# Windowed attention and a squared-ReLU feed-forward: scores by 64-query steps in place of 128-query halves

## The chip, the cores and the metric

One core of a Trainium2 chip runs the whole program. TensorE does the matrix products and writes them to PSUM, ScalarE (ACT) and VectorE (DVE) read PSUM and work between buffers, GpSimd (POOL) and SyncE (SP) issue transfers; a transfer from main memory or a transposing transfer runs on the 16 DMA engines. The metric is the time of one execution on the device in microseconds (us). The kernel before takes 302.01 us (median of 3 runs, 301.80 to 302.15).

## What is computed

Eight sequences with eight heads, 576 positions of 64 numbers. Each query sees the keys at most 32 positions away; the attention output, heads side by side, is the input of a feed-forward layer with a squared ReLU.

```python
B, H, S, D = 8, 8, 576, 64
scores = np.matmul(q, k.transpose(0, 1, 3, 2)) / np.sqrt(D)
scores = np.where(np.abs(pos[:, None] - pos[None, :]) <= 32, scores, -1e9)
attn = softmax(scores)                       # over the keys
x = np.matmul(attn, v)                       # to (B*S, H*D) = (4608, 512)
h = x @ w_in                                 # (512, 2048)
out = np.maximum(h, 0) ** 2 @ w_out          # (2048, 512), float32 out
```

## The kernel before

**Attention by groups.** A group is 192 queries of one sequence, all eight heads; there are 24 groups (`NG`, L15), G = 3 b + g. Its keys are the 256 positions from 32 before to 32 after it. Queries and keys stand transposed in `QT` and `KT`: head dimension on the partitions, heads in four columns `j`, the even head of a pair in partitions 0 to 63 and the odd one (`par`) in 64 to 127. The 256 keys are cut in two halves of 128 (`w`). The 192 queries are three steps of 64: step 0 needs the first key half, step 2 the second, and the middle step needs 64 keys of each.

`scores` (L534) computes, for each key half and head, 128 keys by 128 queries (L565): for `w` = 0 the middle step and then step 0 (an access pattern with a negative step, L564), for `w` = 1 the middle step and then step 2. That is 16 matmuls of 128 columns, in eight pairs: the two of a pair use the lower and the upper 64 rows of the array. From the fourth group on (`NSPLIT = 3`) one block of 16 does both halves and fills all four banks of the PSUM tile `AT`, 1024 columns for each half. ACT takes the exponential of each half, 128 x 1024, into `E` (L589); DVE multiplies it by a band mask of zeros and ones, broadcast over the heads, into `PT` (L594). The masks `MASK[0..3]` are 128 x 128: 1 is the usual second half, 2 and 3 serve the ends of a sequence.

`pv` (L598) multiplies the transposed probabilities by the values: for each key half eight matmuls (L622), one a head, with `PT` as the loaded weights and 65 columns of `V` as the moving operand. Column 64 of `V` is 1, so the sum of the weights comes out beside the result. Head h writes columns `65 * y` to `65 * y + 64` of a bank. Half 0 is divided out for step 0 (DVE L641 and L644, into `XA`), then those rows are set to zero (L650) and half 1 adds to the middle step and makes step 2 (L641 and L644, into `XB`). `VS = 66` is the width in which `V` is stored, two columns of ones.

`xturn` (L652) turns `XA` and `XB` into `XT` with transposing transfers on the SP queue (L717, L720) from group 3 on. The queries and keys of sequences 2 to 7 come by POOL transfers (L394) and are turned by SP transfers (L524); those loads wait for the second P V block of the group three earlier (`gate`, L381).

**The feed-forward.** `mm1` (L725) computes 128 hidden rows by n tokens (192, 256, then 512) in four matmuls each (L737); ACT applies the ReLU (L743) and DVE squares (L746). `mm2` (L750) adds 16 products of 128 x 512 for 128 tokens (L757); ACT moves the result out (L767) and issues the store (L769).

**The order.** Every piece is recorded with its readers and writers, a key and an assumed duration (`Prog.rec`, L96). `schedule` (L127) plays the program through once with these durations: an engine takes, of the pieces that are ready, the one with the lowest key. What it finds is the fixed order in which each engine gets its instructions; on the chip semaphores keep the dependencies. So a changed duration or dependency of one piece can move other pieces, transfers on the queues too. At the start, idle matmuls of zeros (L322) are put into TensorE's gaps.

## Time and profile before

| what | value |
|---|---|
| runs, median | 302.01 us |
| profiled execution, first to last instruction | 299.9 us |
| outside the span (start, end, difference of executions) | 2.1 us |
| TensorE matmul, busy | 291.9 us, 97% |
| DVE, busy | 167.2 us, 56% |
| ACT, busy | 160.3 us, 53% |
| POOL, busy | 107.1 us, 36% |
| DMA engines, mean busy share | nine tenths or more in most of the first 30 of 40 slices |

How to read it: the page has one time per instruction, and "busy" of an engine is the time in which at least one of its instructions is under way. A matmul's time runs to its modelled end, so it holds the passage through the array, and several overlap: a 512-column matmul lasts 379 ns while the next one starts 216 ns after it. What a matmul costs in a row of matmuls is therefore the distance between starts, which the timeline gives: it merges like instructions and shows the start of the first, the time to the end of the last, and their number.

### The profile page before, as it was taken

What the parts mean: (1) busy time and instruction counts of PE and PEld (TensorE: products, weight loads), DVE (VectorE), ACT (ScalarE), POOL (GpSimd) and SP (SyncE); (2) the same over time, 40 slices, a digit from 0 to 9 for tenths busy, and PEclk for the clock granted to TensorE, in tenths of its full rate; (3) what the DMA queues carried; (4) which work ended last, traced back from release to release, by engine and by line L of the source; (5) the groups of instructions that cost most, each with busy time, mean ns of one, the idle gap of its engine ahead of it and who ended that gap; (6) DMA issues with size and microseconds to landing.
All of it is one profiled execution on the core that took longest, in us unless ns stands there. A gap on an engine that the chain in (4) does not pass through costs nothing.

```text
span 299.9 us, 6209 instructions
## 1 busy us (share of the span) xinstructions
PE 291.9 (97%) x2394; PEld 171.8 (57%) x2431; DVE 167.2 (56%) x385; ACT 160.3 (53%) x250; POOL 107.1 (36%) x143
## 2 busy tenths in 40 slices
PE   7899999999999999999999999999999999999996
PEld 3578866848677767664544454444544444444445
DVE  6898775737674767563656666665666632222100
ACT  3497834836467656750765476536744643443312
POOL 8993336503544354455256335533500000000000
PEclk9999999999999999999999999999999999999999
DMA  9999999997999999999999999999992120100112
GB/s 169 176 206 184 196 177 174 169 176 137 164 169 165 95 162 146 155 138 186 180 168 131 114 166 156 125 149 156 154 128 70 55 61 35 37 35 35 38 70 105
DMA packets 160636, 39.83 MB, mean 133 GB/s; under 512 B 149984, under 2 KB 156128, under 8 KB 160608
## 3 DMA queue, kind: packets, MB, share of 16 engines
q0 software_dynamic: 106016, 17.93, 89.3%
q1 hardware_dynamic: 49264, 12.14, 28.5%
q10 hardware_dynamic: 5328, 9.37, 9.1%
q8 instruction: 19, 0.31, 0.5%
q14 instruction: 9, 0.07, 0.1%
HBM read 36.70 MB, written 9.44 MB: 154 GB/s over the span
## 4 chain that ended last, share of the span: by engine, by line
PE 90%; DMA 5%; POOL 3%; issue 1%; ACT 0%; POOLq 0%; ACTq 0%
PE ht L737 41%; PE outp L757 40%; DMA w<-in_moe_w_in_dram 5%; PE at L622 4%; PE at L565 4%; POOL v L443 1%; POOL w L456 1%; PE at L485 1%; PE ht L782 1%; PE outp L782 1%; POOL kpair L426 1%; POOL qpair L426 1%; ACT rt L743 0%; ACT oe L792 0%; POOL dif L325 0%
## 5 line engine op out<-in xcount | busy, mean ns | idle before, releaser
L737 PE MATMUL ht<-xt,w 128*128 128x256 bf16 (+2 forms) x885 | 140.0, 302 | 1.3 <-DMA w<-in_moe_w_in_dram 0.5
L757 PE MATMUL outp<-w,gt 128*128 128x512 bf16 x536 | 133.0, 379 | 1.3
L743 ACT ACTIVATE rt<-ht 128x512 bf16<-128x512 f32 (+1 forms) x152 | 85.9, 578 | 87.1 <-PE ht L737 85.1
L737 PEld LDWEIGHTS ht<-xt,w 128*128 128x128 bf16 x896 | 81.3, 98 | 43.8 <-ACT rt L743 0.6
L746 DVE TENSOR_TENSOR gt<-rt 128x512 bf16<-128x512 bf16 (+1 forms) x152 | 61.5, 408 | 61.6 <-ACT rt L743 60.0
L757 PEld LDWEIGHTS outp<-w,gt 128*128 128x128 bf16 x560 | 51.9, 98 | 54.1 <-ACT oe L767 1.0
L394 POOL DMA_DIRECT2D kraw<-in_k_dram x36 | 27.7, 778 | 107.3 <-PE at L622 56.8
L589 ACT ACTIVATE e<-at 128x1024 bf16<-128x1024 f32 x46 | 44.8, 1021 | 8.7 <-PE at L565 8.4
L594 DVE TENSOR_TENSOR pt<-e,mask 128x1024 bf16<-128x1024 bf16 x46 | 31.8, 691 | 29.0 <-ACT e L589 28.9
L443 POOL DMA_DIRECT2D v<-in_v_dram x48 | 38.2, 809 | 0.0
L767 ACT ACTIVATE oe<-outp 128x512 f32<-128x512 f32 x35 | 21.1, 604 | 29.6 <-PE outp L757 29.6
L394 POOL DMA_DIRECT2D qraw<-in_q_dram x36 | 27.7, 778 | 0.0
L622 PEld LDWEIGHTS at<-v,pt 128*128 128x128 bf16 x384 | 18.3, 98 | 9.9 <-DMA v<-in_v_dram 0.6
L622 PE MATMUL at<-v,pt 128*128 128x65 bf16 x384 | 20.1, 194 | 0.5 <-ACT pt L586 0.5
L644 DVE TENSOR_TENSOR xa<-at,rs 64x512 bf16<-64x512 f32 x24 | 16.7, 695 | 0.9
L644 DVE TENSOR_TENSOR xb<-at,rs 128x512 bf16<-128x512 f32 x24 | 16.5, 689 | 0.7
L565 PEld LDWEIGHTS at<-qt,kt 64*128 64x128 bf16 x384 | 10.8, 94 | 8.7 <-issue 7.1
L565 PE MATMUL at<-qt,kt 64*128 64x128 bf16 x384 | 15.2, 217 | 0.2
L641 DVE RECIPROCAL rs<-at 64x8 f32<-64x8 f32 (+1 forms) x48 | 10.0, 209 | 9.1 <-PE at L622 7.7
L650 DVE MEMSET at<- 64x520 f32 x23 | 11.3, 492 | 3.5 <-DVE xa L644 2.6
L450 DVE COPY v<-v 64x512 bf16<-64x512 bf16 x16 | 5.9, 372 | 5.1 <-PE ht L737 2.9
L789 DVE COPY oe<-ht 128x128 f32<-128x128 f32 x1 | 0.3, 292 | 14.5 <-PE ht L782 14.5
(67 smaller groups left out, 83.2 us busy)
## 6 DMA issues: line engine op xcount, KB each, us to landing
out_dram<-oe ACTq DMA_DIRECT2D x35, 256.0 KB, 3.2
qraw<-in_q_dram POOLq DMA_DIRECT2D x36, 96.0 KB, 5.8
w<-in_moe_w_in_dram POOLq DMA_DIRECT2D x4, 512.0 KB, 10.7
v<-in_v_dram POOLq DMA_DIRECT2D x16, 128.0 KB, 6.6
w<-in_moe_w_out_dram POOLq DMA_DIRECT2D x4, 512.0 KB, 18.8
v<-in_v_dram POOLq DMA_DIRECT2D x16, 96.0 KB, 7.0
kraw<-in_k_dram POOLq DMA_DIRECT2D x12, 112.0 KB, 4.6
kraw<-in_k_dram POOLq DMA_DIRECT2D x12, 96.0 KB, 4.9
```

What stands on the lines that cost most here:

```text
L394: self.p.rec("POOL", lambda e, j=j: e.dma_start(raw[0:h, j, :].rearrange("p (h d) -> p h d", h=8), s[:, j]), writes=[("raw", t, G % NRAW, ...
L443: self.p.rec("POOL", lambda e, j=j, lo=lo, hi=hi, k0=k0: e.dma_start(vt[lo - k0:hi - k0, j, :, 0:64], self.v[b, :, lo:hi, :].rearrange("h ...
L565: mm = e.matmul(sc[:, 512 * par + 128 * j:512 * par + 128 * j + 128], kt[r:r + 64, j, k0:k0 + 128], q, start=G >= NBIAS, stop=True, skip_g ...
L589: self.p.rec("ACT", lambda e, e_=e_, sc=sc: e.activation(e_[:], sc, ACTF.Exp, scale=0.125), reads=tags[w], writes=[("e", n % 2)], key=key, ...
L594: self.p.rec("DVE", lambda e, pt=pt, ee=ee, mb=mb: e.tensor_tensor(pt[:], ee, mb, ALU.mult), reads=[("e", n % 2), ("mask", mi)], writes=[( ...
L622: mm = e.matmul(avp[:, c:c + 65], pt[:, 4 * (h % 2) + h // 2, :], vt[:, w, h, 0:65], start=(w == 0 and y == 0), stop=True, skip_group_chec ...
L644: self.p.rec("DVE", lambda e: e.tensor_tensor(x[r0:128, :].rearrange("p (x y c) -> p x y c", x=2, y=4), av[:, :, :, 0:64], rb, ALU.mult), ...
L737: mm = e.matmul(ht[:, n * x:n * x + n], self.W1[:, ft, 128 * d:128 * d + 128], self.XT[:, ft, r:r + n], start=(ft == 0), stop=(ft == 3))
L743: self.p.rec("ACT", lambda e: e.activation(rt[:, 0:c], ht[:, 0:c], ACTF.Relu), reads=[f"ht{k % 2}"], writes=[("rt", k % 4)], key=key, dur= ...
L746: self.p.rec("DVE", lambda e: e.tensor_tensor(gt[:, d0:d0 + len(ds), r:r + n], rr, rr, ALU.mult), reads=[("rt", k % 4)], writes=[("gt", s, ...
L757: mm = e.matmul(op[:], gt[:, d, r:r + 128], self.W2[:, d, :], start=(d == 0), stop=(d == 15))
L767: self.p.rec("ACT", lambda e: e.activation(oe, op[:], ACTF.Copy), reads=[f"outp{u % 2}"], writes=[("oe", u % 4)], key=key, dur=act(512), n ...
```

## The change

From the fourth group on the scores are computed by `scores_steps` instead of `scores`: for each of the three 64-query steps and each head, the 128 keys of that step by 64 queries. That is 24 matmuls of 64 columns in 12 pairs, steps 0 and 2 into the first two banks of `AT`, the middle step into 256 columns each of the other two. ACT takes two exponentials, 128 x 1024 for steps 0 and 2 (into `E`) and 128 x 512 for the middle step (into `E1`). DVE makes one masked product of 1024 columns, which puts step 0 and step 2 into the right half of their tile of `PT`, and two of 512 columns over 64 partitions, which move the upper and the lower 64 keys of the middle step to the partitions where `pv` wants them: keys 0 to 63 of the middle step go to partitions 64 to 127 of half 0, keys 64 to 127 to partitions 0 to 63 of half 1. `pv` of half 0 now waits for the first product and the first of the small ones, half 1 for the first product and the second small one.

`PT` becomes two buffers with both halves in place of three with one half, used by groups in turn; the four masks become slices of one tensor, so that one access pattern reaches two of them. `pv` uses all 66 columns of `V` in all groups, and the memset of L650 clears 2 x 264 columns in place of 2 x 260. The planner's duration of a score block becomes 590 (`SDUR`), before 660.

```diff
+    def scores_steps(self, G):
...
+        def f(e):
+            for s in (0, 2, 1):
+                for j in range(4):
+                    for par in range(2):
+                        r = 64 * par
+                        c = 512 * par + (1024 + 64 * j if s == 1 else 128 * j + 32 * s)
+                        mm = e.matmul(self.AT[:, c:c + 64], kt[r:r + 64, j, a + 64 * s:a + 64 * s + 128],
+                                      qt[r:r + 64, j, a + 64 * s:a + 64 * s + 64], start=True, stop=True, skip_group_check=True)
+            return mm
...
+        self.moe = self.p.rec("PE", f, reads=rd, writes=lo + hi, key=key, dur=SDUR, name=f"S{G}B")
+        e2, e1, pt = self.E[n], self.E1[n], self.PT[n]
+        self.p.rec("ACT", lambda e: e.activation(e2[:], self.AT[:, 0:1024], ACTF.Exp, scale=0.125), reads=lo, writes=[("e", n)],
+                   key=key, dur=act(1024), name=f"X{G}A")
+        mid = self.AT[:, 1024:2048].rearrange("p (x c) -> p x c", x=2)[:, :, 0:256]
+        self.p.rec("ACT", lambda e: e.activation(e1[:].rearrange("p (x c) -> p x c", x=2), mid, ACTF.Exp, scale=0.125), reads=hi,
+                   writes=[("e1", n)], key=key, dur=act(512), name=f"X{G}B")
+        m0, m2 = 2 if g == 0 else 1, 3 if g == 2 else 1
+        out = bass.AP(pt, 64, [[2048, 128], [128, 8], [1024, 2], [1, 64]])
+        mb = bass.AP(self.MK, 128 * m0 + 64, [[512, 128], [0, 8], [128 * (m2 - m0), 2], [1, 64]])
+        self.p.rec("DVE", lambda e: e.tensor_tensor(out, e2[:].rearrange("p (h s q) -> p h s q", h=8, s=2), mb, ALU.mult),
+                   reads=[("e", n), ("mask", m0), ("mask", m2)], writes=[("pt", n, 0, 0), ("pt", n, 1, 0)], key=key, dur=dve(1024),
+                   name=f"M{G}A")
+        for w in range(2):
+            r, x = 64 * w, 64 * (1 - w)
+            mm = bass.AP(self.MK, r * 512 + 128 + 64, [[512, 64], [0, 8], [1, 64]])
+            self.p.rec("DVE", lambda e, w=w, r=r, x=x, mm=mm: e.tensor_tensor(
+                pt[x:x + 64, w, :, 0:64], e1[r:r + 64, :].rearrange("p (h q) -> p h q", h=8), mm, ALU.mult),
+                reads=[("e1", n), ("mask", 1)], writes=[("pt", n, w, 1)], key=key + 0.01 * w, dur=dve(512), name=f"M{G}m{w}")
...
     def pv(self, G, w):
...
-                c = c0 + 512 * x + 65 * y
-                mm = e.matmul(avp[:, c:c + 65], pt[:, 4 * (h % 2) + h // 2, :], vt[:, w, h, 0:65], start=(w == 0 and y == 0),
+                c = c0 + 512 * x + VS * y
+                mm = e.matmul(avp[:, c:c + VS], pt[:, 4 * (h % 2) + h // 2, :], vt[:, w, h, :], start=(w == 0 and y == 0),
                               stop=True, skip_group_check=True)
...
-        rd = [("v", G % NV, w), ("vset", G % NV), ("pt", n % 3), "zz"]
+        rd = [("v", G % NV, w), ("vset", G % NV), ("pt", G % 2, w, 0), ("pt", G % 2, w, 1), "zz"]
...
-            z = avp[64:128, c0:c0 + 1024].rearrange("p (x c) -> p x c", x=2)[:, :, 0:260]
+            z = avp[64:128, c0:c0 + 1024].rearrange("p (x c) -> p x c", x=2)[:, :, 0:4 * VS]
...
-            for ws in ((0,), (1,)) if G < NSPLIT else ((0, 1),):
+            for ws in ((0,), (1,)) if G < NSPLIT else ():
                 at(3 * G - LEAD + 0.3 * ws[0], self.scores, G, ws)
+            if G >= NSPLIT:
+                at(3 * G - LEAD, self.scores_steps, G)
```

More of the change, by code (lines that the diff above doesn't have):

```diff
@@ L67 @@
 ESPLIT = 0
+SDUR = 590
 IOTA = -1
@@ L297, in alloc @@
         self.DIF = sb("dif", [128, 128], F32)
-        self.MASK = [sb(f"mask{i}", [128, 128], BF16) for i in range(4)]
+        self.MK = sb("mask", [128, 4, 128], BF16)
+        self.MASK = [self.MK[:, i, :] for i in range(4)]
         self.ID = sb("ident", [128, 128], BF16)
         self.E = [sb(f"e{i}", [128, 1024], BF16) for i in range(2)]
-        self.PT = [sb(f"pt{i}", [128, 8, 128], BF16) for i in range(3)]
+        self.PT = [sb(f"pt{i}", [128, 2, 8, 128], BF16) for i in range(2)]
+        self.E1 = [sb(f"em{i}", [128, 512], BF16) for i in range(2)]
         self.RS = [sb(f"rs{i}", [128, 8], F32) for i in range(4)]
@@ L596, in scores @@
                        name=f"M{G}{'AB'[w]}")
+    def scores_steps(self, G):
+        b, g = divmod(G, 3)
+        i = b % 2
+        kt, qt = self.KT[i], self.QT[i]
+        key = 3 * G - LEAD
+        a = 192 * g
+        n = G % 2
+        def f(e):
[7 more added lines that the diff above has]
+            return mm
+        rd = [("qt", i, g)] + [("kt", i, x) for x in range(max(g - 1, 0), g + 1)]
+        rd += [] if b < NTURN else [("qh", i, g)] + [("kh", i, x) for x in range(max(g - 1, 0), g + 1)]
+        rd += [("ktpad", i, 0)] if g == 0 else [("ktpad", i, 1)] if g == 2 else []
+        lo, hi = [self.half(2 * x) + self.half(2 * x + 1) for x in range(2)]
+        self.moe = self.p.rec("PE", f, reads=rd, writes=lo + hi, key=key, dur=SDUR, name=f"S{G}B")
[17 more added lines that the diff above has]
+                reads=[("e1", n), ("mask", 1)], writes=[("pt", n, w, 1)], key=key + 0.01 * w, dur=dve(512), name=f"M{G}m{w}")
@@ L603, in pv @@
         c0 = 1024 * reg
-        vt, pt, avp = self.V[G % NV], self.PT[n % 3], self.AT
+        vt, pt, avp = self.V[G % NV], self.PT[G % 2][:, w], self.AT
         hi, lo = [self.half(2 * reg, x) + self.half(2 * reg + 1, x) for x in (1, 0)]
@@ L611, in f @@
                     x, y = divmod(h, 4)
-                    c = c0 + 512 * x + 65 * y
-                    e.matmul(avp[:, c:c + 65], self.PT[(n - 1) % 3][:, 4 * (h % 2) + h // 2, :], vt[:, 0, h, 0:65], start=(y == 0),
+                    c = c0 + 512 * x + VS * y
+                    e.matmul(avp[:, c:c + VS], self.PT[G % 2][:, 0, 4 * (h % 2) + h // 2, :], vt[:, 0, h, :], start=(y == 0),
                              stop=True, skip_group_check=True)
```

19 lines of the change are left out of this document (10 added, 9 removed).

## The prediction

> **What bounds the kernel now.** I read the page first, then the chain of waits for the start, then TensorE's list of waits, then the timeline around one group.
>
> ```profile
> span 299.9 us, 6209 instructions
> ...
> PE 291.9 (97%) x2394; PEld 171.8 (57%) x2431; DVE 167.2 (56%) x385; ACT 160.3 (53%) x250; POOL 107.1 (36%) x143
> ```
> ```profile
> 10.19 13.79 DMA w<-in_moe_w_in_dram
> 23.98 0.14 issue
> 24.11 1.48 PE ht L737 x16
> ```
> ```profile
> PE ht L737 <- DMA w<-in_moe_w_in_dram: 0.5, 1, 0.5
> PE ht L737 <- ACT rt L743: 0.2, 1, 0.2
> PE ht L737 <- issue: 0.2, 1, 0.2
> ```
>
> The chain (second fence: start, length, what) is held by a weight transfer until 24.11 us; from there TensorE leads. In the list of waits (total, times, longest) its matmuls show after the start only these tenths of a microsecond. A busy share of 97% alone would not prove a full engine, since matmul records overlap; the distances between starts do:
>
> ```profile
> 161.94 1.03 PE L757 MATMUL outp<-w,gt 128*128 128x512 bf16 x4
> 162.90 0.62 PE L565 MATMUL at<-qt,kt 64*128 64x128 bf16 x16
> 163.46 1.90 PE L737 MATMUL ht<-xt,w 128*128 128x512 bf16 x8
> 165.19 1.03 PE L757 MATMUL outp<-w,gt 128*128 128x512 bf16 x4
> 166.06 0.42 PE L622 MATMUL at<-v,pt 128*128 128x65 bf16 x8
> 166.31 1.02 PE L757 MATMUL outp<-w,gt 128*128 128x512 bf16 x4
> ...
> 127.93 1.91 PE L737 MATMUL ht<-xt,w 128*128 128x256 bf16 x16
> 129.68 0.42 PE L622 MATMUL at<-v,pt 128*128 128x65 bf16 x8
> ```
>
> 512 columns cost (165.19 - 163.46) / 8 = 0.216 us, 256 columns (129.68 - 127.93) / 16 = 0.109. So a column costs 0.418 ns and a matmul some 2.5 ns more. The P V block follows its predecessor at once (165.19 + 4 x 0.216 = 166.05) and costs 166.31 - 166.06 = 0.25 to 0.26, 32 ns a matmul. The score block is different: 161.94 + 4 x 0.216 = 162.80, but it starts at 162.90, 0.096 later, and the next matmul comes 163.46 - 162.90 = 0.56 after its start. It costs 0.65 in all. TensorE runs without holes otherwise, so time taken out of these two kinds of block comes off the end, unless a new wait appears.
>
> **The change part by part.**
>
> *Score block.* Rows that count the blocks after 24.11 us (busy, count, of L565 and then of L622):
>
> ```profile
> 24.10:241.00 216.90, 13.03 (x336) 9.42 (x336) 1.00 1.57 149
> ...
> 24.10:241.00 216.90, 18.37 (x352) 16.98 (x352) 1.00 1.57 149
> ```
>
> 336 / 16 = 21 score blocks, which are the groups that change, and 352 / 8 = 44 P V blocks. A score block's last start lies 0.62 less one matmul (0.217, the page's row below) after its first, 0.40, and 0.56 - 0.40 = 0.16 passes from there to the next block; the windows view gives the 0.40 as pairs:
>
> ```profile
> 162.89:162.92 0.03, 0.02 (x2) 0.02 (x4) 1.00 1.81 188
> 162.92:162.96 0.04, 0.04 (x2) 0.04 (x4) 1.00 1.78 195
> 162.96:163.01 0.05, 0.05 (x4) 0.05 (x6) 1.00 1.84 238
> ...
> L565 PE MATMUL at<-qt,kt 64*128 64x128 bf16 x384 | 15.2, 217 | 0.2
> ```
>
> In the first 0.03 us two matmuls and four weight loads have started, and no third matmul before 162.96. So the halves of the array run together, and a pair takes (0.62 - 0.217) / 7 = 57 ns, the price of 128 columns once (128 x 0.418 + 2.5 = 56). What is left of the 0.65 is the way into and out of the half-array mode: 0.65 - 8 x 0.057 = 0.19. I keep 0.19.
>
> A pair of 64 columns is not in the trace. By the slope it costs 64 x 0.418 + 2.5 = 29 ns; the nearest row is this transpose of 64 columns, each with its own load:
>
> ```profile
> 30.09 0.29 PE L696 MATMUL at<-ident,xa 64*128 64x64 bf16 x4
> ...
> L696 PE MATMUL at<-ident,xa x8: 190/190/200, 23.0 to 30.2; 64*128 64x64 bf16 x8
> ```
>
> (0.29 - 0.19) / 3 = 33 ns, with the slower first start in it. P V, 32 ns with a full 128-row load, says the same. Bounds: 26.7 ns (columns without the constant) and 33 ns; an end far outside, no shortening at all, is rival 1. I take 29. The block becomes 0.19 + 12 x 0.029 = 0.54, a gain of 0.65 - 0.54 = 0.106 (0.19 + 8 x 0.057 = 0.646 unrounded), in 21 blocks 2.23 us; between the bounds 1.3 and 2.8. The 168 further loads cost nothing as long as they run under the matmuls: four in the first 0.03 us, against four per 0.029 wanted.
>
> The Trainium skill (TensorE: Matmul & The Clock Gate, section Back-to-back issue gap) speaks against such small matmuls: from 1 to 64 columns one costs about 60 cycles, its issue floor of about 25 ns. By that, applied to each of 24 matmuls, the estimate is a block of 0.19 + 0.60 = 0.79 instead of 0.54. The rows above do not agree that halves of a pair pay it apart, since two start within 0.03 us and the third 0.05 later.
>
> *P V in 66 columns.* The slope gives 65 x 0.418 + 2.5 = 29.7 ns, the trace 32. Outputs begin at column 65 y, so four of eight at an odd one, and all are odd in width; I read the 2.3 ns as the price of the odd width. With 66 all begin even: 66 x 0.418 + 2.5 = 30.1, a gain of 0.015 per block, 44 x 0.015 = 0.65 us. If the 2.3 ns have another cause, a column more costs 8 x 0.42 = 3 ns, 0.15 us in all: bounds 0.70 gained, 0.15 lost. I take 0.65. The memset of L650 gets 8 more elements in some 492 ns of DVE time that nothing waits for; no term.
>
> *Exponential and mask.* ACT's second exponential shrinks to 512 columns; DVE gets one product more.
>
> ```profile
> 163.56 1.94 ACT L589 ACTIVATE e<-at 128x1024 bf16<-128x1024 f32 x2 [0.76 <-PE at L565]
> 164.62 0.69 DVE L594 TENSOR_TENSOR pt<-e,mask 128x1024 bf16<-128x1024 bf16 x1 [1.36 <-ACT e L589]
> ...
> 165.54 0.69 DVE L594 TENSOR_TENSOR pt<-e,mask 128x1024 bf16<-128x1024 bf16 x1 [0.22 <-ACT e L589]
> ```
> ```profile
> L743 ACT ACTIVATE rt<-ht 128x512 bf16<-128x512 f32 x120 | 70.6, 600 | 76.8 <-PE ht L737 75.3 <-DVE pt L594 0.8 <-DVE gt L746 0.5
> ...
> L746 DVE TENSOR_TENSOR gt<-rt 128x512 bf16<-128x512 bf16 x120 | 50.7, 424 | 59.1 <-ACT rt L743 58.1
> ...
> L644 DVE TENSOR_TENSOR xa<-at,rs 64x512 bf16<-64x512 f32 x24 | 16.7, 695 | 0.9
> ```
>
> ACT: 1.02 becomes 0.60 (L743's mean for the same size), 21 x 0.42 = 8.8 us less on an engine that is 53% busy. DVE: 0.69 becomes 2 x 0.424 (L746), 21 x 0.16 = 3.3 us more on one that is 56% busy. Neither is on the path by its total. What counts is the new wait: P V of half 0 now needs the second exponential too. Today its product ends at 164.62 + 0.69 = 165.31, and P V starts at 166.06, 0.75 spare. After: the block ends 0.106 earlier, the exponentials start at 163.45 and the second ends at 163.45 + 0.92 + 0.60 = 164.97; the large product, from 164.51 to 165.20, is by then at work, so the small one starts at some 165.15 and ends near 165.6; P V's place is 166.06 - 0.11 = 165.95. Spare 0.35. In the instruction order of the changed kernel at least twelve 512-column matmuls (12 x 0.216 = 2.59) stand between a score block and its first P V, the same least distance as before, so this group stands for the tight ones. Half 1 is less pressed: its last product ends near 165.95 in place of 166.23. Behind a waiting P V stands all of TensorE, so what the chain is later than 0.35 is paid 21 times: rival 2. The exponential over two pieces of 256 lies between 0.60 and the old 1.02; at the far end 0.42 - 0.35 = 0.07 x 21 = 1.5 us would be lost. I take 0.60.
>
> *Order, queues, buffers.* No transfer is added or removed. Up to the fifth group's first P V block TensorE's order is the same; later the planner swaps neighbouring pieces of feed-forward and P V, and some turning transfers on SP, in both directions. `PT` and `E` are reused after two groups, later than now. The loads on POOL wait for the P V block three groups earlier and so come earlier with it; what doesn't shrink is a transfer's time: rival 3.
>
> *Sum.* 2.23 + 0.65 = 2.88 us off the path. The profiled execution's span of 299.9 becomes 297.0; the 2.1 us between it and the runs' median stay: 302.01 - 2.88 = **299.1 us**.
>
> **The rivals.**
>
> 1, slower: *the halves take turns.* 16 matmuls with their loads start in 0.40 us, which is also 25 ns each; if that is a price of each load or issue and the 57 ns of a pair are two of them, only the number counts. The block gains nothing from narrow columns except 27 ns at its end, and loses 8 x 25 = 200: +0.173 x 21 = 3.6 us, with P V's gain 302.01 + 3.6 - 0.65 = 305.0. It decides from 38 ns a pair on (8 x 57 / 12). Against it: two starts within 0.03 us and 33 ns or less for 64 columns with a load. For it: no four instructions per 29 ns are seen over a whole block.
>
> 2, slower: *the products lose their fast rate.* They write and read runs of 64 and cross partitions. L644, 512 columns from PSUM at 695, against L746's 424 shows the price: about 0.53 ns more a column. The large product is 0.54 later, the small 0.27, less 0.35 spare: 0.46 x 21 = 9.7, hence 302.01 - 2.88 + 9.7 = 308.8. Small products alone (0.27) stay hidden. Against: 0.69 for 1024 and 0.424 for 512 lie on one line although the runs are 128 and 512 long.
>
> 3, no change: *the transfers set the pace.*
>
> ```profile
> 215.97 1.24 SPq L524 DMA_TRANSPOSE kt<-kraw  x1
> ...
> DMA to landing us min/median/max: 2.3/5.2/8.3
> ...
> 223.44 0.62 PE L565 MATMUL at<-qt,kt 64*128 64x128 bf16 x16
> ```
>
> This block's last turned keys were issued 7.5 us before it and take 5.2 in the middle, 8.3 at worst: little is spare here. Between the gate and the block lie three groups, 3 x (0.106 + 0.03) = 0.41 us gained; were nothing spare, each third group would give them back, 7 x 0.41 = 2.9: 302.0. Against: no matmul waits for a turned tile now. One or two late landings would cost 0.4 each.
>
> **How the numbers follow.** Forecast 83%, rival 1 5%, rival 2 4%, rival 3 in full 4%, something else slower 4%. The forecast's own bounds: 302.01 - 2.8 - 0.70 = 298.5 at best; 302.01 - 1.3 + 0.15 = 300.9 at worst, and the late exponential or a few late landings end in the same place. 298.4 to 301.0 holds it and leaves out 17%. A change of 0.2% (0.6 us) is what a measurement tells from none: faster 83%, within 4%, slower 13%.
>
> **What would show it.** Right: 24 score matmuls in a group whose time from first start to end falls from 0.62 to 11 x 0.029 + 0.19 = 0.51; P V blocks at 30 ns, 0.41 long; no waits of TensorE on DVE at P V; small products near 0.42. Wrong: score groups of 0.8 us (rival 1), waits of P V on the product (2) or on turned tiles (3).

## The result, and the profile after

The changed kernel takes 301.28 us (median of 19 executions, 300.81 to 302.74), the kernel before, run beside it on the same chip, 302.07 us (19 executions, 301.68 to 302.44). The ratio is 0.9984, with a 95% interval of 0.9976 to 0.9992: faster, by 0.8 us between the medians, where 2.9 were forecast. Its executions lie 1.9 us apart, with a tail towards longer times, and those of the kernel before 0.8; so the means differ by only 0.5 us, and the ratio lies near theirs. Three executions of *e8_copy* and one of *e14_all2* that were over 1.5% longer than the fastest of their kernel stand in none of the figures below.

First the page of the changed kernel: the span, the busy times, and the rows of the instructions that are new (busy, mean ns of one, idle before). Line numbers (L634) are those of the kernel whose profile is shown; the memset L650 of the kernel before is L696 in the changed one, P V is L622 and L668.

```profile
span 299.1 us, 6567 instructions
...
PE 290.5 (97%) x2562; PEld 170.5 (57%) x2599; DVE 170.6 (57%) x406; ACT 151.8 (51%) x250; POOL 107.1 (36%) x143
...
L634 DVE TENSOR_TENSOR pt<-e,mask 128x1024 bf16<-128x1024 bf16 x21 | 14.5, 693 | 24.1 <-ACT e L626 24.1
...
L640 DVE TENSOR_TENSOR pt<-em,mask 64x512 bf16<-64x512 bf16 x42 | 17.6, 420 | 1.3
...
L629 ACT ACTIVATE em<-at 128x512 bf16<-128x512 f32 x21 | 12.5, 597 | 0.0
```

The large product still takes 693 ns, a small one 420, the exponential over 512 columns 597. ACT has 8.5 us less to do, DVE 3.4 more; the forecast had 8.8 and 3.3. None of these durations is the cause of the miss. Then TensorE's timeline around one group of the changed kernel, for the score block (start, length, what, number of instructions):

```profile
110.88 1.91 PE L783 MATMUL ht<-xt,w 128*128 128x256 bf16 x16
112.72 0.52 PE L616 MATMUL at<-qt,kt 64*128 64x64 bf16 x24
113.17 1.92 PE L783 MATMUL ht<-xt,w 128*128 128x256 bf16 x16
```

Read as in the prediction: the sixteen matmuls before it give the block free at 110.88 + 16 x 0.109 = 112.62, it starts 0.10 later, and the next start is 0.45 after its own. That is 0.55 in all, where the forecast had 0.54 and the kernel before had 0.65. From the starts of single matmuls in the trace the median over the 21 blocks is 552 ns, 649 before: 96 into the half-array mode, 330 from the first pair to the last (eleven distances, 30.0 in the mean), 126 from the start of the last pair to the next matmul. 97 ns x 21 = 2.04 us were gained here, and 2.23 were forecast.

The P V block, in the same view:

```profile
162.98 0.42 PE L668 MATMUL at<-v,pt 128*128 128x66 bf16 x8
...
163.24 1.89 PE L783 MATMUL ht<-xt,w 128*128 128x512 bf16 x8
```

163.24 - 162.98 = 0.26, as before. Nothing was gained of the 0.65 us that were forecast for the 66 columns.

The remaining difference is waits that the kernel before does not have. The first kind, in group 8 of the changed kernel (DVE and TensorE; in brackets the idle time before a group and what ended it):

```profile
84.03 0.69 DVE L634 TENSOR_TENSOR pt<-e,mask 128x1024 bf16<-128x1024 bf16 x1 [0.49 <-ACT e L626]
...
84.75 0.87 DVE L640 TENSOR_TENSOR pt<-em,mask 64x512 bf16<-64x512 bf16 x2
...
85.66 0.43 DVE L792 TENSOR_TENSOR gt<-rt 128x512 bf16<-128x512 bf16 x1
86.11 0.21 DVE L687 RECIPROCAL rs<-at 64x8 f32<-64x8 f32 x1
...
86.36 0.29 DVE L453 COPY v<-v 64x512 bf16<-64x512 bf16 x1
86.67 0.69 DVE L690 TENSOR_TENSOR xa<-at,rs 64x512 bf16<-64x512 f32 x1
...
87.40 1.03 PE L803 MATMUL outp<-w,gt 128*128 128x512 bf16 x4
87.40 0.43 DVE L792 TENSOR_TENSOR gt<-rt 128x512 bf16<-128x512 bf16 x1
...
87.94 0.50 DVE L696 MEMSET at<- 64x528 f32 x1
...
88.49 0.43 PE L668 MATMUL at<-v,pt 128*128 128x66 bf16 x8
```

TensorE is free for the second P V block at 87.40 + 4 x 0.216 = 88.26. The memset that clears the rows of half 0 ends at 88.44, and P V starts at 88.49: 0.23 us lost, measured from the starts (the view names no releaser for so short a wait). DVE has hardly a hole in this stretch. In the kernel before the same memset was done well ahead:

```profile
87.09 0.49 DVE L650 MEMSET at<- 64x520 f32 x1
...
87.62 0.43 DVE L746 TENSOR_TENSOR gt<-rt 128x512 bf16<-128x512 bf16 x1
...
88.48 0.42 PE L622 MATMUL at<-v,pt 128*128 128x65 bf16 x8
```

It ends at 87.58, 0.9 before P V. Two things have moved it: DVE has one product more in front, and the square of the feed-forward that came behind the memset (87.62) now stands in front of it (87.40). Group 11 repeats the picture of the changed kernel, again 0.23. A third wait of 0.33 us stands at 200.4, where ACT hands over an output bank late:

```profile
198.35 1.89 PE L803 MATMUL outp<-w,gt 128*128 128x512 bf16 x8
...
199.75 0.60 ACT L813 ACTIVATE oe<-outp 128x512 f32<-128x512 f32 x1 [2.64 <-PE outp L803]
...
200.41 0.82 PE L803 MATMUL outp<-w,gt 128*128 128x512 bf16 x3 [0.17 <-ACT oe L813]
```

This one does not come from the order. *e1_pv65* below has the same order there and no such wait:

```profile
198.73 2.75 PE L803 MATMUL outp<-w,gt 128*128 128x512 bf16 x12
...
199.79 0.60 ACT L813 ACTIVATE oe<-outp 128x512 f32<-128x512 f32 x1 [2.30 <-PE outp L803]
```

The copy starts 1.06 us after the product is taken up again, in the changed kernel 1.40. It has two things to wait for, TensorE's last matmul for the bank and an old store from its buffer, which had landed 25 us earlier in both kernels. In the changed kernel a separate waiting instruction of ACT stands for TensorE, which signals at 199.39, and the copy itself waits for the store: it starts 0.36 us behind the signal. In *e1_pv65* the copy itself waits for TensorE, and starts 0.02 behind the signal (199.77). Why the first form costs so much here is not shown.

With shorter waits, some 0.2 together, that makes 1.0 us. The first product behind the chain of the start begins 0.19 later (24.30 against 24.11); in the profiles of *e2_psum128*, *e8_copy* and *e11_sp*, which open with the same instructions, it begins at 23.99, 24.19 and 24.81. So for the two profiled executions: -2.04 + 1.0 + 0.2 = -0.8 us, which is the difference of the spans, 299.9 and 299.1.

What the profiled execution of the changed kernel shows only as an edge is a fourth place, near 61 us: there P V starts at 61.60, at the moment at which TensorE is free. The copy of V for group 8 (`copy_v`, which waits for the V transfer of group 7) now stands on DVE in front of group 5's memset, and P V waits for that memset. In the kernel before the copy stood behind it, and waited there while no product of TensorE waited for it:

```profile
59.81 0.49 DVE L650 MEMSET at<- 64x520 f32 x1
61.26 0.29 DVE L450 COPY v<-v 64x512 bf16<-64x512 bf16 x1 [0.95 <-DMA v<-in_v_dram]
```

In the stretch from 44 to 70 us the DMA engines are busy nine tenths or more in both kernels, but for one slice of the changed one (the DMA row of that window, 40 slices of 44 to 86 us; before, then after):

```profile
DMA  9999999999999999999999999244799999969999
```
```profile
DMA  9999999999999949999999999436699999936999
```

The V transfer that the copy waits for took 9.1 us from issue to landing in this execution, and 11.0 to 11.8 in the profiles of *e2_psum128*, *e5_smallmid*, *e6_margins* and *e7_v72*; in those four P V waits here for 1.2 to 1.9 us. In the kernel before it took 11.5, and nothing of TensorE waited. The experiments ask three things: what the steps of P V cost and why, what the three waits behind DVE and ACT are worth, and whether transfers make the executions differ.

### The profile page after: what moved, and what is told of

Its sections match the earlier page's. It is cut to its first block, busy times and chain, and to the rows that moved or that the text cites. A ratio compares the mean times of both kernels' runs of the same rounds, so it can differ in the third digit from the quotient of the medians.

```text
span 299.1 us, 6567 instructions
## 1 busy us (share of the span) xinstructions
PE 290.5 (97%) x2562; PEld 170.5 (57%) x2599; DVE 170.6 (57%) x406; ACT 151.8 (51%) x250; POOL 107.1 (36%) x143
## 4 chain that ended last, share of the span: by engine, by line
PE 86%; DMA 5%; POOL 3%; DVE 3%; issue 2%; ACT 1%; ACTq 0%; POOLq 0%
PE outp L803 39%; PE ht L783 38%; DMA w<-in_moe_w_in_dram 5%; PE at L668 4%; PE at L616 3%; POOL v L446 1%; POOL w L459 1%; PE at L488 1%; ACT e L626 1%; PE ht L828 1%; PE outp L828 1%; POOL qpair L429 1%; DVE pt L640 1%; POOL kpair L429 1%; DVE xa L690 0%
## 5 line engine op out<-in xcount | busy, mean ns | idle before, releaser
L803 PE MATMUL outp<-w,gt 128*128 128x512 bf16 x535 | 131.6, 379 | 1.8 <-issue 0.5
L803 PEld LDWEIGHTS outp<-w,gt 128*128 128x128 bf16 x560 | 52.9, 98 | 57.7 <-ACT oe L813 1.9
L634 DVE TENSOR_TENSOR pt<-e,mask 128x1024 bf16<-128x1024 bf16 x21 | 14.5, 693 | 24.1 <-ACT e L626 24.1
L626 ACT ACTIVATE e<-at 128x1024 bf16<-128x1024 f32 x21 | 21.4, 1021 | 11.9 <-PE at L616 11.9
L668 PEld LDWEIGHTS at<-v,pt 128*128 128x128 bf16 x384 | 17.9, 98 | 10.8 <-DVE at L696 2.1
L668 PE MATMUL at<-v,pt 128*128 128x66 bf16 x384 | 20.1, 194 | 0.7 <-DMA v<-in_v_dram 0.5
L640 DVE TENSOR_TENSOR pt<-em,mask 64x512 bf16<-64x512 bf16 x42 | 17.6, 420 | 1.3
L696 DVE MEMSET at<- 64x528 f32 x23 | 11.5, 498 | 3.3 <-DVE xa L690 2.0
L616 PEld LDWEIGHTS at<-qt,kt 64*128 64x128 bf16 x504 | 8.5, 95 | 7.3 <-issue 6.3
L629 ACT ACTIVATE em<-at 128x512 bf16<-128x512 f32 x21 | 12.5, 597 | 0.0
L616 PE MATMUL at<-qt,kt 64*128 64x64 bf16 x504 | 11.0, 191 | 0.0
## 6 DMA issues: line engine op xcount, KB each, us to landing
w<-in_moe_w_in_dram POOLq DMA_DIRECT2D x4, 512.0 KB, 11.5
```

The source lines that it names most:

```text
L616: mm = e.matmul(self.AT[:, c:c + 64], kt[r:r + 64, j, a + 64 * s:a + 64 * s + 128], qt[r:r + 64, j, a + 64 * s:a + 64 * s + 64], start=Tru ...
L626: self.p.rec("ACT", lambda e: e.activation(e2[:], self.AT[:, 0:1024], ACTF.Exp, scale=0.125), reads=lo, writes=[("e", n)], key=key, dur=ac ...
L640: self.p.rec("DVE", lambda e, w=w, r=r, x=x, mm=mm: e.tensor_tensor(pt[x:x + 64, w, :, 0:64], e1[r:r + 64, :].rearrange("p (h q) -> p h q" ...
L668: mm = e.matmul(avp[:, c:c + VS], pt[:, 4 * (h % 2) + h // 2, :], vt[:, w, h, :], start=(w == 0 and y == 0), stop=True, skip_group_check=True)
L803: mm = e.matmul(op[:], gt[:, d, r:r + 128], self.W2[:, d, :], start=(d == 0), stop=(d == 15))
```

## The experiments

Each kernel is told by its difference from the changed kernel or from the kernel before; ratios are to the kernel before, run beside it.

**P V: width, place of the output, place of V.** The steps between the eight starts of a P V block are, in both kernels, 29, 35, 33, 33, 29, 33, 33 ns (medians over 49 blocks). The prediction put what lies above 30 down to the odd width.

*e1_pv65*: the changed kernel with 65 columns again (the instructions of DVE that read or clear the result follow), all else kept. Three points in a cut of code stand for what is left out.

```diff
-                c = c0 + 512 * x + VS * y
-                mm = e.matmul(avp[:, c:c + VS], ..., vt[:, w, h, :], ...
+                c = c0 + 512 * x + 65 * y
+                mm = e.matmul(avp[:, c:c + 65], ..., vt[:, w, h, 0:65], ...
```

> The changed kernel with P V in 65 columns again, all else and every engine's order as in it. Theory A (the width is worth nothing: in both traces a P V block takes 0.256 us, with the same steps of 29, 35, 33, 33 ns): within 0.3 us of the changed kernel, P V blocks still 0.256. Rival (66 columns do save the 0.015 us per block that I forecast, and something else hides it): 0.65 us slower than the changed kernel.

301.20 us (300.10 to 302.47; 0.9972, interval 0.9956 to 0.9988), and the steps stay as they are, within 1 ns. Odd width and odd output columns cost nothing; the column more costs nothing either.

*e2_psum128*: outputs of the heads at columns 0, 128, 256, 384 of a bank.

```diff
-                c = c0 + 512 * x + VS * y
+                c = c0 + 512 * x + 128 * y
```

> The changed kernel with the P V outputs at every 128th column of a bank instead of every 66th; widths and orders as in it. Theory A1 (the 3 to 5 ns over the 29 come from where an output begins in PSUM, since the first of each bank takes 29): all steps 29 to 30 ns, a block 0.235 to 0.240, 0.7 us faster than the changed kernel. Rival A2 (they come from the moving operand or the loads, which are unchanged): steps stay, time within 0.2 us.

302.16 us (300.68 to 304.31; 1.0004, 0.9988 to 1.002), steps 29, 35, 32, 33, 29, 33, 33. The place of the output in its bank is not it. The time is 0.9 us above the changed kernel's, where at most 0.2 were expected, although no instruction of TensorE or DVE became longer; its profiled execution lost 1.60 us at P V near 61 us, the fourth place above.

*e7_v72* and *e10_before72*: the rows of `V` and their ones 72 columns apart (144 bytes, a multiple of 16) in place of 66 (132 bytes), with 66 columns moved in the changed kernel and 65 in the kernel before. The outputs stay where they were.

```diff
-VS = D_ + 2
+VS = D_ + 8
...
```

> The changed kernel with each head's row of V stored 72 columns apart instead of 66, 66 columns moved as before; outputs and orders as in it. Theory A3 (the steps of 29, 35, 33, 33 ns follow where the moving operand begins: heads 0 and 4 begin at multiples of 16 bytes and take 29, the others do not; 72 columns are 144 bytes, so all begin at such a multiple): all steps 29 to 30 ns, a block 0.238 instead of 0.256, in 44 blocks 0.7 us faster than the changed kernel when that is not held up. Rival (weight loads or the number of columns): steps and time as in the changed kernel.

> The kernel before with each head's row of V stored 72 columns apart, 65 columns moved; orders as in it. Theory A3: a P V block takes 0.237 instead of 0.256, 44 x 0.019 = 0.8 us faster than the kernel before, near 301.3. Rival (loads, or an effect of the new scores): as the kernel before.

The steps become 29, 35, 29, 29, 29, 30, 35 in both kernels. TensorE's timeline of the kernel before with rows 72 apart:

```profile
105.85 0.41 PE L622 MATMUL at<-v,pt 128*128 128x65 bf16 x8
106.10 1.24 PE L757 MATMUL outp<-w,gt 128*128 128x512 bf16 x5
```

The block takes 0.245 in place of 0.256 (medians of the starts; 106.10 - 105.85 shows it to a hundredth), 0.011 x 44 = 0.5 us. The kernel before falls to 301.47 us (301.19 to 302.56; 0.9983, 0.9974 to 0.9992). The changed kernel shows 301.19 (299.86 to 302.11; 0.9967, 0.9951 to 0.9982) with a wait of 1.20 us at 61 in its profiled execution: there the gain is hidden behind the spread (its lowest time of 299.86 is no proof, since *e1_pv65*, which gains nothing at P V, has 300.10). With the way to the next matmul, 33 ns before and 29 now, a block has eight distances; five were of 33 ns, of which four fall to 29 or 30 and one rises to 35. They were the price of where the moving operand starts, and that is in `V`, not in PSUM.

*e12_before96*: the kernel before with rows 96 apart (192 bytes, a multiple of 64).

```diff
-VS = D_ + 2
+VS = D_ + 32
```

> The kernel before with the rows of V and their ones laid 96 columns apart (192 bytes) in place of 65, 65 columns moved by each small product as before. With rows 72 apart (144 bytes) the steps of a P V block were 29, 35, 29, 29, 29, 30, 35 ns and the block 0.245 us. Theory 64-byte lines (a start off a multiple of 64 bytes still costs in two places): all seven steps become 29 to 30 ns, the block 0.235 us, and the time falls by another 0.010 x 44 = 0.45 us below that kernel's 301.47, to about 301.0 us. Rival, the two steps of 35 ns belong to something else (the order of the row and column parts, or the output): they stay and the time is 301.3 to 301.7 us.

Steps 29, 35, 29, 29, 29, 29, 35: a start at a multiple of 64 bytes brings nothing over one at a multiple of 16. The time is 301.99 (301.96 to 303.38; 1.001, 0.9999 to 1.0021), no gain at all, although its P V blocks take 0.245 as with rows 72 apart. The loss lies in the opening. DVE sets the ones behind the values at the start; rows of that line for the first 24 us of the kernel before and of this one:

```profile
L372 DVE MEMSET v<- 128x32 bf16 x6 | 0.5, 85 | 0.0
```
```profile
L372 DVE MEMSET v<- 128x512 bf16 x6 | 2.9, 485 | 0.3
```

2.4 us more of DVE, at a time when DVE prepares the first queries and keys; TensorE's block behind the first turned results starts at 24.55 us in place of 24.11 (23.86 with rows 72 apart). From that block to its last matmul the kernel takes 272.95 us, and the one with rows 72 apart 272.95 as well. So what the rows gave is lost before 24.55. That the longer memsets are the cause fits, but no run of its own shows it: openings of the same instructions differ as much (above), though seven of the eleven executions lie within 0.05 us of the profiled one. What the two steps of 35 ns are stays open.

**The scores, and whether TensorE sets the end.** *e13_scores2x*: each of the 12 pairs issued twice, the second writing the same result again.

```diff
-            for s in (0, 2, 1):
+            for s in (0, 2, 1, 0, 2, 1):
```

> The changed kernel with each of the 12 pairs of 64-column score products issued twice (the second writes the same result over the first). Theory, TensorE sets the end one for one: 12 pairs x 30.1 ns x 21 blocks = 7.6 us more, 308.5 to 309.2 us. Rival, transfers or the exp and mask chain set the end in the 21 blocks: clearly less than that, under 305 us.

```profile
115.61 0.88 PE L616 MATMUL at<-qt,kt 64*128 64x64 bf16 x48
116.42 1.92 PE L783 MATMUL ht<-xt,w 128*128 128x256 bf16 x16
```

A block of 48 takes 902 ns (median), 350 more than one of 24: 29.2 ns for each further pair. 21 x 0.350 = 7.35 us; the span is 6.9 longer (306.0) and the median 6.5 (307.79, two executions). That is 0.7 below the expected range and 2.8 above the rival's bound: TensorE sets the end nearly one for one, and the score term of the forecast is right. 0.45 to 0.85 us come back; in the profile the waits of 0.23, 0.23 and 0.33 are down to 0.14, 0.14 and none, which is 0.5.

**The waits behind DVE and ACT.** *e5_smallmid*: the two small products take 8 of the 64 queries of the middle step, the other 56 are left as they were, so the middle step's result is not computed. The order is the same, DVE has less to do.

```diff
-            mm = bass.AP(self.MK, r * 512 + 128 + 64, [[512, 64], [0, 8], [1, 64]])
+            mm = bass.AP(self.MK, r * 512 + 128 + 64, [[512, 64], [0, 8], [1, 8]])
...
-   pt[x:x + 64, w, :, 0:64], e1[r:r + 64, :].rearrange("p (h q) -> p h q", h=8), mm, ALU.mult)
+   pt[x:x + 64, w, :, 0:8], e1[r:r + 64, :].rearrange("p (h q) -> p h q", h=8)[:, :, 0:8], mm, ALU.mult)
```

> The changed kernel with the two small mask products cut to 8 of 64 queries (the other 56 of the middle step are left out, so their probabilities are stale); orders as in it. Theory A (1.0 us of the gain came back as TensorE waits; two of 0.24 us at the second P V block of the ninth and twelfth group, because the second small product delays reciprocal, normalisation and memset on DVE): those two waits go, 0.3 to 0.5 us faster than the changed kernel. Rival B (transfers set the pace): no change beyond 0.2 us, waits on transfers instead.

300.84 us (300.59 to 302.54; 0.9975, 0.9959 to 0.999). The waits of P V in groups 8 and 11 fall from 0.23 to 0.06 us each, the one for ACT stays. Seven of its twelve executions lie within 0.33 us of each other, five are 0.9 to 1.6 us above them. The profiled one is of the five, and P V waits 1.20 us in it near 62 us, behind the copy of V. So taking the work of the small products away takes the two waits away, and leaves the spread.

*e6_margins*: the planner counts 0.25 us more behind each memset of half 0 and behind each output copy. No instruction changes, only the order.

```diff
-  ... writes=hi, key=key - 0.05, dur=495, name=f"Z{G}")
+  ... writes=hi, key=key - 0.05, dur=495, name=f"Z{G}").lat += 250 * (G >= NSPLIT)
-  ... key=key, dur=act(512), name=f"o{u}")
+  ... key=key, dur=act(512), name=f"o{u}").lat += 250
```

> The changed kernel, planned with 0.25 us more from the memset of the P V rows, and from the copy of a feed-forward result, to whoever waits for them, so that the order leaves them more room; no instruction is changed. Theory A (the order set these waits): the waits of 0.24, 0.24 and 0.34 us go, about 0.8 us faster than the changed kernel, near 300.4. Rival B (transfers set the pace): same time, TensorE waits elsewhere.

300.59 us (299.86 to 302.07; 0.9953, 0.994 to 0.9967), 0.7 below the changed kernel; the three waits of 0.79 us in all are down to two of 0.04 and 0.07. Its profiled execution is its longest, and shows what is left (DVE, then TensorE):

```profile
62.38 0.29 DVE L453 COPY v<-v 64x512 bf16<-64x512 bf16 x1 [2.17 <-DMA v<-in_v_dram]
62.79 0.50 DVE L696 MEMSET at<- 64x528 f32 x1
```
```profile
63.34 0.43 PE L668 MATMUL at<-v,pt 128*128 128x66 bf16 x8 [1.72 <-DVE at L696]
```

The copy waits 2.17 us for its transfer, the memset stands behind the copy, P V behind the memset. TensorE loses 1.9 us at once.

**The late transfers.** *e8_copy*: the copy of V for group 8 has to wait for group 5's memset; on every engine the order is otherwise the same.

```diff
-                   after=self.moe if G >= VCS else None)
+                   after=self.p.named['Z5'] if G == 8 else self.moe if G >= VCS else None)
```

> The changed kernel with one instruction moved: the copy of 64 rows of V for the ninth group, which waits for a transfer, comes behind the memset of the sixth group's P V rows on DVE, as before the change, instead of in front of it. Theory D (executions differ by up to 1.9 us because this transfer's landing decides when that memset, and through it the second P V block, can start): no TensorE wait near 61 us, executions between 300.7 and 301.3, median near 301.0. Rival (the spread comes from the opening's transfers or elsewhere): the spread of 300.8 to 302.7 stays.

A miss: 302.68 us (300.26 to 304.68; 1.001, 0.9984 to 1.0035). No wait is left at 61 us in its profiled execution, of 304.68, but TensorE's timeline shows another:

```profile
68.38 0.42 PE L668 MATMUL at<-v,pt 128*128 128x66 bf16 x8
71.15 2.50 PE L783 MATMUL ht<-xt,w 128*128 128x256 bf16 x16 [2.36 <-issue]
```

The product of tokens 768 to 1023 needs the turned result of step 0 of group 5 (`xt<-xa`). SP's queue in this kernel, and that transfer's time from issue to landing:

```profile
61.76 1.30 SPq L527 DMA_TRANSPOSE qt<-qraw  x1
63.10 1.25 SPq L763 DMA_TRANSPOSE xt<-xa  x1
```
```profile
xt<-xa SPq DMA_TRANSPOSE x1, 8.0
```

63.10 + 8.0 = 71.1, and the product starts at 71.15. In the kernel before the same transfer is issued nearly 4 us earlier; SP's queue of the kernel before and of the changed one:

```profile
56.28 2.57 SPq L524 DMA_TRANSPOSE kt<-kraw  x2
59.34 2.16 SPq L717 DMA_TRANSPOSE xt<-xa  x1
```
```profile
57.08 3.47 SPq L527 DMA_TRANSPOSE kt<-kraw  x2
60.59 1.44 SPq L527 DMA_TRANSPOSE qt<-qraw  x1
62.07 1.25 SPq L763 DMA_TRANSPOSE xt<-xa  x1
```

Before, it was behind two turning transfers of keys; now a turning transfer of q has been put ahead of it, and in the changed kernel it goes out 2.7 us later, while TensorE wants it only 1.1 us later (the timelines have the first of the 256-column products at 68.7 us, and before at 67.6). In the profiled execution of the changed kernel it took 5.0 us and came 1.6 before its use. With the 7.4 us that it took in the kernel before, where it still came 0.9 ahead, it would be late here, and with 8.0 it is.

*e11_sp*: e8_copy, and on SP the two turning transfers of q of group 7 moved behind those of x of group 5.

```diff
+        late = [p.named['tdq210'], p.named['tdq211']]
+        p.ops = [o for o in p.ops if o not in late]
+        x = p.ops.index(p.named['T5b']) + 1
+        p.ops[x:x] = late
```

> The kernel with the copy of V for group 8 behind group 5's memset, and on SP's queue the two turning transfers of q of group 7 moved behind the turning transfer of x's second half of group 5; the order on every other engine stays. Theory transfers late (in the kernel with the moved copy the turning transfer of group 5's second half of x was issued at 65.73 us, and the first 256-wide product of the block, L783, stood until 71.15 us for it, a wait of 2.52 us): it is issued near 63.1 us, the wait falls to 0.5 us or less, the executions lie at 300.2 to 301.3 us. Rival, the spread comes from elsewhere (the opening, or the raw loads): the wait goes, or was not what made the slow executions, and they stay spread over 300.3 to 305.4 us.

(The expectation names the second half of x; by the rows above it was the first that came last. The move puts both ahead of q.) 301.16 us (300.27 to 302.34; 0.9973, 0.996 to 0.9987), 1.5 below e8_copy's median. The wait that ended at 71.15 us is gone, but its profiled execution waits at the next turned tile:

```profile
74.89 1.26 SPq L766 DMA_TRANSPOSE xt<-xb  x1
```
```profile
81.04 1.02 PE L803 MATMUL outp<-w,gt 128*128 128x512 bf16 x4
82.91 1.03 PE L783 MATMUL ht<-xt,w 128*128 128x256 bf16 x8 [0.85 <-issue]
```

That transfer took 7.9 us to land, 74.89 + 7.9 = 82.8. So the place was named rightly, while the spread stayed 2.1 us: behind the one late transfer stood the next.

*e16_fewv* and *e17_before_fewv*: the V transfers of groups 6 to 12 cut to their last 8 rows, in the changed kernel and in the kernel before; the other rows keep what an earlier group left there, so these groups' results are not the attention. Every instruction and order is kept.

```diff
-                vt[lo - k0:hi - k0, j, :, 0:64], self.v[b, :, lo:hi, :] ...
+                vt[(hi - 8 if 6 <= G <= 12 else lo) - k0:hi - k0, j, :, 0:64], self.v[b, :, hi - 8 if 6 <= G <= 12 else lo:hi, :] ...
```

> The changed kernel with the transfers of V for groups 6 to 12 cut to their last 8 rows (the other rows keep what an earlier group left there); every instruction and every order as in the changed kernel. Theory transfers: with that much less to move between 38 and 100 us no product waits for a transfer at 61 to 82 us, the executions lie within 0.8 us, and the median is 299.9 to 300.6 us (lowest 300.6 of the changed kernel less a few tenths). Rival, the spread is made by orders on the engines or by the opening: 300.8 to 302.7 us as before.

> The kernel before with the same seven V transfers cut to 8 rows (the other rows keep what an earlier group left there). Theory: in the kernel before no product waits for a transfer after the start, so nothing is gained: 301.8 to 302.2 us. Rival, transfers hold TensorE in the kernel before as well, where the list of waits does not show it: 301.5 us or less.

The changed kernel: 300.73 us (300.52 to 301.15 in five executions; 0.9952, 0.994 to 0.9964), 0.1 above the range of the expectation, and narrow, as the theory of late transfers has it. The copy of V no longer waits, and the memset is done in time:

```profile
60.40 0.50 DVE L697 MEMSET at<- 64x528 f32 x1
```
```profile
61.20 0.42 PE L669 MATMUL at<-v,pt 128*128 128x66 bf16 x8
```

The waits behind DVE in groups 8 and 11 are still there (0.32 and 0.26 us); the one of 0.33 behind ACT is not, its copy waits as in *e1_pv65*. The kernel before gains nothing: 302.05 (301.82 to 302.49; 0.9995, 0.9986 to 1.0004). So transfers cost the changed kernel up to 0.55 us in the median (0.2 if the wait behind ACT is taken off) and 1.6 in its longest execution (302.74 against 301.15), and the kernel before nothing clear of noise.

**Together.** *e9_all* and the same kernel again as *e15_all*: the changed kernel with the margins of e6, the moved copy of e8 and the rows of e7.

> The changed kernel with three edits: planned with 0.25 us more room behind the memset of the P V rows and behind the copy of a result, the V copy of the ninth group behind the sixth group's memset, and V stored 72 columns apart. Theory A with A3 and D: score blocks give 2.0 us, P V 0.7, and hardly any waits are left: 302.05 - 2.7 = 299.3 to 299.8, with a spread under 0.8 us. Rival B (transfers set the pace): no better than 300.5.

> The kernel with the margins behind Z and behind the copies of results, rows of V 72 apart and the moved copy of V, as e9_all, for more executions. Theory orders (the margins and the moved copy have removed the waits): median 299.3 to 299.9 us, executions within 1 us. Rival, transfers of the stretch from 44 to 85 us are late in some executions whatever the order: median 299.6 to 300.4 us, single executions up to 302 us.

299.58 us (299.16 to 300.00; 0.9914, 0.9901 to 0.9926) and 299.60 us (299.45 to 300.10; 0.9915, 0.9902 to 0.9928): 1.7 us below the changed kernel, and eight executions on two chips within 0.94 us. It beats both kernels. In the profile of *e15_all* no matmul after 31 us starts more than 0.02 us late.

*e14_all2* adds e11's move on SP, *e18_m72* leaves out the moved copy:

```diff
 e18_m72
-                   after=self.p.named['Z5'] if G == 8 else self.moe if G >= VCS else None)
+                   after=self.moe if G >= VCS else None)
```

> The kernel with all three edits (0.25 us of margin behind Z and behind the copies of results, the copy of V moved, rows of V 72 apart: 299.58 us) and besides it the two turning transfers of q moved behind that of x on SP. Theory transfers late: 299.2 to 299.8 us, and the executions lie within 0.8 us of each other. Rival, that place no longer waits with the margins: the same time, and a spread that is no narrower.

> The changed kernel with the margins behind Z and behind the copies of results and with rows of V 72 apart; the copy of V for group 8 stays in front of group 5's memset. Theory: the wait of P V at 61 us stays in most executions (0 to 1.9 us), median 300.0 to 300.5 us, spread 299.3 to 301.6. Rival, the moved copy only moves the wait on to the turned tiles: the same median as with the moved copy, within 0.3 us.

e18_m72: 300.89 us (299.75 to 301.74; 0.9952, 0.9936 to 0.9969), 1.3 above e15_all beside it, more than either theory said. With the margins in place the moved copy is worth that, in eight executions against four; alone, in e8_copy, it only passed the wait on. e14_all2: 299.96 us (299.18 to 302.08; 0.9946, 0.9928 to 0.9964): the move on SP brings nothing there, and the spread is back, so the theory that predicted executions within 0.8 us missed. Its profile, of a short execution, has no late transfer that could say why. Why the turned tiles come late in e8_copy and e11_sp and not in e9_all and e15_all, whose order on SP puts q ahead of x as in the changed kernel, isn't settled; eight executions may also be too few to meet one.

## Why the prediction was wrong

The sign was right; 2.88 us were forecast and 0.79 measured (302.07 - 301.28). The 2.1 that are missing divide about as follows, with each part from its own measurement.

**The score block: right, 0.19 us too much.** Pairs run together, a pair costs 30.0 ns where 29 were taken, and the way in and out is as it was. Rival 1, halves in turn, needed 38 ns. The rule of the Trainium skill that stood against it (TensorE: Matmul & The Clock Gate, section Back-to-back issue gap: about 60 cycles for 1 to 64 columns) would have made the block an estimated 0.79; the trace has 0.552, so for pairs on the two halves of the array the trace does not agree with it.

**P V in 66 columns: wrong, 0.65 us.** The failed step is "I read the 2.3 ns as the price of the odd width". It was a guess at a cause from two facts that came together, width and output column. The change takes the odd width away, e1 puts it back, e2 moves the output, and nothing changes; e7, e10 and e12 show where 0.5 us of it lies, in the distance of the rows of V, which the change left at 66. The other bound, 0.15 lost, was nearer, though the column more cost nothing either.

**The spare of half 1: wrong, about 0.7 us with the wait for ACT.** The prediction says "Half 1 is less pressed" because its own last product ends early. That looked at one chain only. The second P V block also waits for the memset behind half 0's result, of which the prediction says that it is "DVE time that nothing waits for"; and on DVE the second small product stands in front of that chain: reciprocal, normalising, memset. The spare was read off one group near 164 us; groups 8 and 11 are tighter. Their waits are 0.46 us in the profile. The 0.33 for ACT come on top; they hang on which of two waits the copy itself holds, which the prediction did not look at and which differs between kernels of the same order. Together that is 0.79 in the profile and 0.7 between the medians of the changed kernel and e6.

**Transfers: rival 3 in part, 0.2 to 0.55 us.** It had 4 in 100 "in full", looked at the turned keys of a late group, and priced a late landing at 0.4 us. What came late, in the profiles of experiments, were the V transfer of group 7 and the turned results of groups 5 and 6, all between 60 and 83 us, at 1.0 to 2.5 us each. The sentence that failed is the one on order, in which the prediction put at nothing what new neighbours on a queue cost: "later the planner swaps neighbouring pieces of feed-forward and P V, and some turning transfers on SP, in both directions", at no cost. Two swaps could be tied to late landings: the copy of V ahead of group 5's memset on DVE, and a turning transfer of q ahead of that of x on SP. The square ahead of group 8's memset is a third of the kind, without a transfer.

0.19 + 0.65 + 0.7 + 0.55 = 2.1 us. That this fits so well is luck: the last two are differences of medians of kernels whose executions lie 0.6 to 2.2 us apart, and the wait behind ACT may be counted in both. The firmer sum comes from the other side, from the combination without waits: the 2.04 of the score blocks and the 0.5 of the rows of V give 302.07 - 2.04 - 0.5 = 299.5, measured 299.6.

**Right as forecast:** the durations on ACT and DVE (rival 2 had the products 0.54 and 0.27 us longer), and that P V of half 0 keeps its place behind the new products: no wait of TensorE for them stands in the changed kernel's list.

## What to carry to other kernels

Where every order comes out of a plan, a change that makes a stage faster is also a new plan: list what each queue now puts in front of the pieces that others wait for, and price that, above all where a transfer's landing stands in the queue of a busy engine. A spare is that of the whole chain of dependencies, through every engine that it crosses, in the tightest group. When the shape of an operand is suspected, its distances in memory, its width and its output can each be changed alone, in a few lines.

## What the runs showed of the hardware

A small matmul with full loads costs 29 or 30 ns for 65 or 66 columns in six of eight places of a block, and 35 in two, when its moving operand starts at multiples of 16 bytes (rows 144 or 192 bytes apart); where rows lie 132 bytes apart, five of the eight cost 33. Multiples of 64 add nothing, and neither the width's parity nor the output's start in its bank matters (e1, e2, e7, e10, e12). In a run of pairs on the two halves of the array a further pair of 64 columns costs 29.2 ns (e13), and some 96 pass before the first pair starts.

The clock after a wait of TensorE: in e8_copy, windows with busy times, and behind them the granted clock, the DMA share and GB/s:

```profile
69.00:71.00 2.00, 0.00 (x0) 0.00 (x0) 1.23 (x3) 0.00 (x0) 0.00 (x0) 1.00 1.50 91
71.00:73.00 2.00, 1.85 (x14) 1.56 (x15) 0.15 (x1) 0.60 (x1) 0.00 (x0) 0.83 1.11 284
73.00:75.60 2.60, 2.60 (x16) 1.36 (x14) 0.70 (x2) 0.80 (x2) 0.00 (x0) 0.50 0.21 40
```

After 2.5 us without a start the first matmuls still run at full rate; from 72.3 to 75.7 us the clock is 0.50, and the distances between starts double, 213 ns for 256 columns. That costs another 1.6 us (the excess of those distances, summed). That the wait brings it about fits, but one profile is all there is: behind the waits of 1.2 to 1.9 us in the profiles of e5, e7, e2 and e6 the clock stayed at 1.00. The Trainium skill (TensorE: Matmul & The Clock Gate, section What's actually happening) has half rate after an idle window of about 3.4 us, counted by a free-running window. This trace agrees with the half rate, and its 3.4 us are as long as that window; the gap here was shorter than the window.
